# Streamed weights of a two-layer attention and mixer kernel: held output blocks, a shorter ring, and key and query loads in two transfers

## The chip, the cores and the metric

The kernel runs on one core of a Trainium2 chip. The metric is the device time of one execution in microseconds, the median of three runs. The profile is that of one execution, taken by the hardware profiler, and it is a little longer (3707.0 us) than the timed runs.

## The reference

A sequence of 2048 rows with 640 columns passes through attention, a mixer, and both a second time with the same weights. Each block adds its result to its input.

The attention block works on 64 segments of 32 rows, one after the other, with 8 memory rows ahead of each:

```
for s in range(n_seg):                     # 64 segments
    h = concat([mem, x[32 s : 32 s + 32]]) # 8 + 32 rows of 640
    q, k, v = h @ Wq, h @ Wk, h @ Wv       # 32 heads of 192 columns
    p = softmax(mask(q k^T * scale))
    o = (p v) @ Wo                         # 6144 -> 640
    mem = o[:8]                            # the next segment's memory
    outs.append(o[8:])
```

The memory rows of a segment are an output of the segment before, so the segments of one block can't be computed side by side. Wq, Wk, Wv and Wo have 640 x 6144 elements each, 7.9 MB in bfloat16, 31.5 MB together, and every segment needs all of them.

The mixer normalizes, multiplies by w1 (640 x 640), applies gelu, shifts four groups of columns by one or two rows up or down, multiplies by w2 (640 x 640), normalizes, multiplies by w3 (640 x 1536), applies gelu and multiplies by w4 (1536 x 640).

## The kernel before

**Steps and lanes.** The first attention (lane 0) and the second (lane 1) use the same weights, so the kernel runs them together: step t handles segment t of lane 0 and segment t - 5 of lane 1 (`LAG`). There are 69 steps. A step's activations hT are 2 x 40 = 80 columns wide. Each weight block is loaded into TensorE once per step and multiplied with these 80 columns. Every second step a chunk of the mixer (64 rows of both lanes) is worked off in between.

**Groups.** The 32 heads go in 8 groups of 4 (768 columns). For each group there is a projection of keys and of queries (`proj_kq`, 5 blocks of 128 rows each, 6 matmuls a block, line 526), one of values (`proj_v`, line 567, with a transposition at L579), then `attend`: scores (L598), softmax on VectorE and ScalarE, transposition (L631), product with the values (L646), copy to oT (L652), and the output projection (L663), 6 blocks of 5 matmuls, which adds into the tile psy. When all 8 groups have been added, L701 copies the memory rows out of psy into the next step's hT.

**Resident and streamed weights.** `CUT` says how many blocks of each group stay in SBUF for the whole run. Keys, queries and values keep 3 of 5 blocks in each group. The output weights keep 2, 4, 4, 4, 4, 4, 2, 2 of 6. The other blocks are streamed again in every step, two blocks to a load, into a ring of buffers of 128 x 1536 elements (`wst`). The ring has 10 buffers (`RING`). Attention may hold 9 (`RING_A`) and the mixer's weights, which are all streamed, 3 (`RING_B`). `block` (line 415) makes the attention loads: a resident one at L425, a streamed one at L435. `load_b` makes the mixer's at L459. All are issued by the SP queue, in order. SP waits before each load until TensorE has freed the buffer.

**The order of the work.** A planner in Python (`Plan.place`) orders everything by hand before the program is built. Each operation has an engine, a cost and a due time, and the planner puts at each point the operation that can start first and is due first. It also models the ring, with a rate, a latency and a skew of the loads (`DMA_RATE`, `DMA_LAT`, `DMA_SKEW`). A planned step is 48 us long (`STEP`). So a constant of the planner changes the order of instructions on every engine, and nothing else.

**Held output blocks.** The end of a step is a chain: the last groups' softmax, their output projection, the memory rows, and only then the next step's first keys. To give TensorE work in it, the output projections of groups 2 to 6 can be kept back: oT has 7 buffers (`OT_BUFS`), and the due time of these groups is the step's end (line 655). In the kernel before this holds for resident blocks alone. A streamed block is due two group lengths after its group began (line 671).

Of the kernel before, what the change touches and what calls it, by code (L numbers as in the profile page):

```python
# [19 lines left out]

LAG = 5
HG = 4
RING = 10
RING_A = 9
RING_B = 3
CUT = {"k": [3] * 8, "q": [3] * 8, "v": [3] * 8, "o": [2] + [4] * 5 + [2] * 2}
YA = 3
STEP = 48.0
PSUM_BANKS = {"y": 2, "x": 6}
PSUM_USES = {"y": ("y", 2), "P": ("x", 4), "S": ("x", 3), "B": ("x", 2)}  # L30
OT_BUFS = 7
# [4 lines left out]
LOOK = 0.03  # L36
DMA_RATE = 345.0e3
DMA_LAT = 2.2
DMA_SKEW = 2.8


class Buf:
# [194 lines left out]
def kernel(  # L237
# [16 lines left out]
    nc = tc.nc  # L254
    P = 128
# [6 lines left out]
    KC = Dm // P  # L262
    FC = F // P
    assert (Dm, F, Dh, H, SEG, M) == (640, 1536, 192, 32, 32, 8) and S % (2 * SEG) == 0 and NSEG > 8
    NG = H // HG
    GW = HG * Dh
    GC = GW // P
# [108 lines left out]
    add = plan.add  # L376
# [9 lines left out]
    def T(b):  # L386
        if b.obj is None:
            b.obj = b.make()
        return b.obj

    def mm_us(n, m=128, k=1):
        return k * (max(min(64, m), n) / 2400.0 + 0.0025)
# [9 lines left out]
    def w_src(kind, g, a, e):  # L402
        if kind == "o":
            return Wo_v[:, g, a:e, :]
        return W_v[kind][:, a:e, GW * g:GW * (g + 1)]
# [9 lines left out]
    def block(t, kind, g, c, due):  # L415

        n = Dm if kind == "o" else GW
        cut = CUT[kind][g]
        if c < cut:
            if (kind, g) not in resident:  # L420
                tl = wres.tile([P, cut, n], bf16, name=f"w{kind}{g}")
                b = Buf()

                def fn(op):
                    nc.sync.dma_start(out=tl[:], in_=w_src(kind, g, 0, cut))  # L425
                add("SP", 0.45, due, fn, w=(b,), dma=P * cut * n * 2, queue="wa")
                resident[kind, g] = b, tl
            b, tl = resident[kind, g]
            return b, lambda: tl[:, c, :]
        a = cut + (c - cut) // 2 * 2  # L430
        if (t, kind, g, a) not in streamed:
            b = ring("ra")

            def fn(op):
                nc.sync.dma_start(out=T(b)[:, 0:2 * n].rearrange("p (c n) -> p c n", c=2), in_=w_src(kind, g, a, a + 2))  # L435
            add("SP", 0.45, due, fn, w=(b,), dma=P * 2 * n * 2, queue="wa")
            streamed[t, kind, g, a] = b
        b = streamed[t, kind, g, a]
        return b, lambda: T(b)[:, (c - a) * n:(c - a + 1) * n]
# [62 lines left out]
    def attention_step(t):  # L502
# [3 lines left out]
        N = NS if both else L1  # L506
        maskt = mask2[:] if both else (mask_a if 0 in ln else mask_b[:])
        base = t * STEP
        sl = STEP / NG
# [77 lines left out]
        def attend(g):  # L587
            G = t * NG + g
            s0 = base + sl * g
            q, k_, V_ = qT[G % 2], kT[G % 2], Vt[G % V_BUFS]  # L590
# [60 lines left out]
            def f7(op):  # L651
                nc.vector.tensor_copy(out=o_[:, :, 0:N], in_=T(pso)[:, :, 0:N])  # L652
            add("DVE", dve_us(GC * N), hi - 4, f7, r=(pso,), w=(B("oT", G % OT_BUFS),))
            ws = [block(t, "o", g, c, s0 + (1.9 if g < NG - 1 else 1.2) * sl + 0.03 * c) for c in range(GC)]
            due = base + STEP - 1 + 0.02 * g if g >= NG - OT_BUFS + 1 else s0 + 2.0 * sl

            def out_rows(m0, m1, c0_, c1_, j):

# [7 lines left out]
            if g < NG - 1:  # L666
                for c in range(GC):
                    def f8(op, c=c):
                        out_rows(0, YA, c, c + 1, 0)()
                        out_rows(YA, KC, c, c + 1, 1)()  # L670
                    add("PE", mm_us(N, k=KC), due if c < CUT["o"][g] else s0 + 2.0 * sl, f8,
                        r=(ws[c][0], B("oT", G % OT_BUFS)), a=tuple(psy))
            else:
                for j, (m0, m1) in enumerate(((0, YA), (YA, KC))):
                    def f8(op, j=j, m0=m0, m1=m1):
                        out_rows(m0, m1, 0, GC, j)()
                    add("PE", mm_us(N, k=GC * (m1 - m0)), due + 0.5 * j, f8,
                        r=(*{id(b): b for b, _ in ws}.values(), B("oT", G % OT_BUFS)), a=(psy[j],))
# [5 lines left out]
        g = NG - 2  # L684
# [7 lines left out]
        due = base + STEP - 5  # L692
# [11 lines left out]
        for j, (k0, k1) in enumerate(((0, YA), (YA, KC))):  # L704
            def fy(op, j=j, k0=k0, k1=k1):
# [5 lines left out]
                a=() if j == 0 else (B("yTB", t % 2),))  # L711
# [123 lines left out]
    def chunk(c):  # L835
# [108 lines left out]
            gelu(pz, e - a, i, due, outs, (B("hTB", i),))  # L944
        hs = [ps("B", [XB, HC], f32, "hs") for _ in range(2)]
        for n in range(5):
            due = D(0.4 + 0.04 * n)
            wb, wv = load_b(c, "w2", n, due)

            def fw(op, n=n, wv=wv):  # L950
                w = wv()
                off = W2OFF[n] if n < 4 else 0
                lhsT = hTB[:, n, off:off + TOK, :].rearrange("p w l -> p (w l)")
                for k in range(2):
                    nc.tensor.matmul(out=T(hs[k])[:], lhsT=lhsT, rhs=w[:, HC * k:HC * (k + 1)],  # L955
                                     start=hs[k].begin(), stop=True, skip_group_check=True)
            add("PE", mm_us(HC, k=2), due, fw, r=(wb, B("hTB", 0), B("hTB", 1)), a=tuple(hs))
# [19 lines left out]
        for i in range(4):  # L977
            a, e = 3 * i, 3 * i + 3
            pz = ps("B", [P, 3, XB], f32, "psh2")
            for n in range(a, e):  # L980
                due = D(0.7 + 0.04 * n)
                wb, wv = load_b(c, "w3", n, due)

                def fw(op, n=n, a=a, wv=wv, pz=pz):
                    w, o = wv(), T(pz)
                    for kc in range(KC):
                        nc.tensor.matmul(out=o[:, n - a, :], lhsT=w[:, kc * P:(kc + 1) * P],  # L987
                                         rhs=vT[:, kc, 0:XB], start=(kc == 0), stop=(kc == KC - 1))
                add("PE", mm_us(128, k=KC), due, fw, r=(wb, vTk), a=(pz,))
            gelu(pz, 3, i % 2, due, [(0, P, 0, 3, h2T[:, a:e, :])], (B("h2T", i),))  # L990

    def chunk_end(c):
        base = (2 * c + 2) * STEP
        D = lambda x: base + x * STEP
        xk, vk = B("xw"), B("vb")
        s4k = B("st", 3)
        y2 = [ps("B", [XB, HC], f32, "y2") for _ in range(2)]
        for n in range(FC):
            due = D(1.2 + 0.03 * n)
            wb, wv = load_b(c, "w4", n, due)  # L1000

            def fw(op, n=n, wv=wv):
                w = wv()
                for k in range(2):
                    nc.tensor.matmul(out=T(y2[k])[:], lhsT=h2T[:, n, :], rhs=w[:, HC * k:HC * (k + 1)],  # L1005
                                     start=y2[k].begin(), stop=True, skip_group_check=True)
            add("PE", mm_us(HC, k=2), due, fw, r=(wb, *(B("h2T", k) for k in range(4))), a=tuple(y2))
        for k in range(2):
            def fs(op, k=k):
                cs = slice(HC * k, HC * (k + 1))  # L1010
                nc.vector.scalar_tensor_tensor(out=xo[:, cs], in0=T(y2[k])[:], scalar=0.5, in1=xw[:, cs],
                                               op0=ALU.mult, op1=ALU.add)
            add("DVE", dve_us(HC), D(1.5), fs, r=(y2[k], xk), w=(B("xo"), B("fin")) if k == 0 else (),
                a=() if k == 0 else (B("xo"), B("fin")))
        for lane in range(2):
            w0 = rows_of(c, lane)
            a, b = max(0, -w0), min(TOK, S - w0)
            if b <= a or a >= TOK:
                continue

            def fst(op, lane=lane, a=a, b=b, w0=w0):
                dst = x2d if lane == 0 else outd
                nc.gpsimd.dma_start(out=dst[w0 + a:w0 + b, :], in_=xo[2 * a + lane:2 * b:2, :])
            add("POOL", 0.9, D(1.55), fst, r=(B("xo"),), w=(B("x2d", c),) if lane == 0 else (), dma=(b - a) * Dm * 2)
        segs = [(2 * c - 1, 0, 2, 30, "xc"), (2 * c, 2, 2 + SEG, 0, "xa"), (2 * c + 1, 2 + SEG, TOK, 0, "xb")]
        segs = [x for x in segs if 0 <= x[0] < NSEG]
        if segs:
            st_ = st4[3]
            ln_ops(xo, XB, st_, s4k, B("xo"), D(1.5), False)
            apply_ln(vb, xo, XB, st_, 0, vk, B("xo"), s4k, D(1.5), 0.45)  # L1030
            ps4 = ps("B", [P, KC, XB], bf16, "psn")
            transposes(ps4, vb, XB, D(1.5), (vk,))
            for (sg, a, b, o0, key) in segs:
                tt = sg + LAG

                def fc(op, a=a, b=b, o0=o0, tt=tt):
                    pv = T(ps4)[:].rearrange("p k (w l) -> p k l w", l=2)
                    d0 = L1 + M + o0
                    nc.scalar.copy(out=hT[tt % 4][:, :, d0:d0 + b - a], in_=pv[:, :, 0, a:b])
                add("ACT", act_us(KC * (b - a)), D(1.55) + (0.0 if o0 else 1.0), fc, r=(ps4,), w=(B("hT", tt % 4, key),))  # L1040
        if c + 1 < NCH:
            chunk_loads(c + 1)
# [81 lines left out]
```

## Time and profile before

| | before |
|---|---|
| median of 3 runs | 3685.22 us (3682.99 to 3686.92) |
| span of the profiled run | 3707.0 us |
| TensorE matmul busy | 3410.3 us (92%), 84,703 matmuls |
| VectorE, ScalarE, GpSimd busy | 2362.8, 1710.7, 308.2 us |
| moved by DMA | 1141.77 MB, mean 308 GB/s |
| of it by the SP queue | 1113.63 MB |
| streamed attention loads | 759 output, 552 key, 552 query, 552 value |
| mixer loads | 630 |
| median time of a streamed load from issue to landing | 5.5 to 5.9 us |

Busy time of TensorE is a modelled figure, since matmuls overlap, so 92% doesn't say that it runs at its peak. A wait is listed as engine, line, what ended it, then the sum in us, the number of waits and the longest one. "Issue" is put where the engine stood still and the profile shows nothing that it waited for. A queue's share of 16 engines is the time of its packets divided by 16 times the span.

### The profile page before, as it was taken

The page shows a single profiled execution, that of the slowest core. Times are in us where ns is not written, and L with a number is a line of the kernel's source. Part 1 is how long each engine was busy: PE and PEld are TensorE (multiplying, and loading weights), DVE is VectorE, ACT ScalarE, POOL GpSimd, SP SyncE. Part 2 cuts the span into 40 slices and gives each one's busy share as a digit, 9 for nine tenths or more (in the row PEclk, how much of TensorE's full clock was granted, in tenths as well). Part 3 has the DMA queues.
Part 4 walks back from the last instruction along what each step waited for, and adds up shares of the span by engine and source line. Part 5 has one row for each costly group of instructions (what it writes and reads, how often), then busy time and mean ns, then how long its engine had stood idle before and what let it go on. Part 6 is the DMA issues. An engine that isn't in the chain of part 4 may idle for free.

```text
span 3707.0 us, 188581 instructions
## 1 busy us (share of the span) xinstructions
PE 3410.3 (92%) x84703; PEld 3273.5 (88%) x84703; DVE 2362.8 (64%) x7085; ACT 1710.7 (46%) x3584; POOL 308.2 (8%) x522
## 2 busy tenths in 40 slices
PE   5889999999999999999999999999999999999896
PEld 4778999999999999999998999988999999898785
DVE  2455666766666666666666666666666667666455
ACT  1344444444444544444444445444445445444333
POOL 2000000000000000000000000000000000000000
PEclk9999999999999999999999999999999999999898
DMA  9999999999999998999999999999899999999996
GB/s 343 320 305 303 311 313 308 307 307 305 316 307 322 321 313 296 304 311 317 305 308 304 318 310 307 313 307 309 291 314 318 311 306 309 298 315 313 298 322 217
DMA packets 841818, 1141.77 MB, mean 308 GB/s; under 512 B 54190, under 2 KB 837564, under 8 KB 841008
## 3 DMA queue, kind: packets, MB, share of 16 engines
q1 hardware_dynamic: 832496, 1113.63, 90.6%
q0 software_dynamic: 8512, 16.08, 1.2%
q8 instruction: 662, 10.85, 1.2%
q14 instruction: 148, 1.21, 0.1%
HBM read 1124.25 MB, written 8.19 MB: 305 GB/s over the span
## 4 chain that ended last, share of the span: by engine, by line
PE 88%; issue 7%; DMA 3%; ACT 1%; DVE 1%; SPq 0%; POOL 0%; POOLq 0%; DVEq 0%; ACTq 0%
PE psq L526 16%; PE psk L526 15%; PE psy L663 15%; PE psv L567 15%; PE psvt L579 5%; PE pss L598 4%; PE pso L646 4%; PE psh L987 3%; PE y L1005 3%; PE pst L631 2%; DMA wst<-in_A_Wq_dram 1%; PE psh L933 1%; PE hs L955 1%; DMA wst<-in_A_Wv_dram 1%; ACT V L583 1%
## 5 line engine op out<-in xcount | busy, mean ns | idle before, releaser
L652 DVE CAST oT<-pso 128x480 bf16<-128x480 f32 (+1 forms) x552 | 340.9, 618 | 396.6 <-PE pso L646 393.1
L526 PEld LDWEIGHTS <-wst 128*128 128x128 bf16 x13248 | 548.6, 100 | 47.4 <-issue 30.1
L583 ACT COPY V<-psvt 80x768 bf16<-80x768 bf16 (+1 forms) x552 | 438.5, 794 | 298.9 <-PE psvt L579 298.3
L526 PE MATMUL psq<-hT,wq 128*128 128x80 bf16 (+1 forms) x9936 | 475.9, 199 | 51.2 <-issue 21.2
L526 PE MATMUL psk<-hT,wk 128*128 128x80 bf16 (+1 forms) x9936 | 474.6, 199 | 38.8 <-issue 29.8
L573 ACT CAST vTs<-psv 128x480 bf16<-128x480 f32 (+1 forms) x552 | 292.0, 529 | 458.4 <-PE psv L567 458.0
L567 PE MATMUL psv<-hT,wv 128*128 128x80 bf16 (+1 forms) x9936 | 481.0, 199 | 18.7 <-issue 17.1
L609 DVE CUSTOM_DVE_ANT_1 pss<-pss,mask 80x320 f32<-80x320 f32 (+1 forms) x512 | 245.8, 480 | 380.2 <-PE pss L598 376.5
L534 ACT CAST qT<-psq 128x480 bf16<-128x480 f32 (+1 forms) x552 | 292.7, 530 | 405.4 <-PE psq L526 404.0
L526 PEld LDWEIGHTS <-wq 128*128 128x128 bf16 x9936 | 411.1, 100 | 69.3 <-issue 49.4
L526 PEld LDWEIGHTS <-wk 128*128 128x128 bf16 x9936 | 400.7, 100 | 45.8 <-issue 40.6
L663 PE MATMUL psy<-oT,wo 128*128 128x80 bf16 (+1 forms) x8970 | 414.6, 199 | 24.1 <-issue 17.5
L567 PEld LDWEIGHTS <-wv 128*128 128x128 bf16 x9936 | 402.9, 100 | 34.7 <-issue 21.9
L636 ACT COPY PT<-pst 80x320 bf16<-80x320 bf16 (+1 forms) x552 | 221.8, 402 | 385.3 <-PE pst L631 377.3
L663 PE MATMUL psy<-oT,wst 128*128 128x80 bf16 (+1 forms) x7590 | 379.1, 199 | 20.7 <-issue 16.0
L663 PEld LDWEIGHTS <-wo 128*128 128x128 bf16 x8970 | 358.4, 100 | 35.2 <-issue 26.0
L567 PE MATMUL psv<-hT,wst 128*128 128x80 bf16 (+1 forms) x6624 | 356.8, 199 | 21.5 <-issue 19.2
L526 PE MATMUL psk<-hT,wst 128*128 128x80 bf16 (+1 forms) x6624 | 346.7, 200 | 19.0 <-issue 13.9
L621 DVE TENSOR_REDUCE sm<-pss 80x4 f32<-80x320 f32 (+1 forms) x552 | 252.6, 458 | 172.4 <-ACT pss L616 171.7
L663 PEld LDWEIGHTS <-wst 128*128 128x128 bf16 x7590 | 317.9, 100 | 37.0 <-issue 24.9
L526 PE MATMUL psq<-hT,wst 128*128 128x80 bf16 (+1 forms) x6624 | 324.1, 199 | 16.0 <-issue 11.6
L542 DVE CAST kT<-psk 128x320 bf16<-128x320 f32 (+1 forms) x552 | 253.7, 460 | 122.1 <-PE psk L526 121.4
(117 smaller groups left out, 5285.2 us busy)
## 6 DMA issues: line engine op xcount, KB each, us to landing
wst<-in_A_Wo_dram SPq DMA_DIRECT2D x759, 320.0 KB, 5.5
wst<-in_A_Wk_dram SPq DMA_DIRECT2D x552, 384.0 KB, 5.9
wst<-in_A_Wq_dram SPq DMA_DIRECT2D x552, 384.0 KB, 5.7
wst<-in_A_Wv_dram SPq DMA_DIRECT2D x552, 384.0 KB, 5.7
wst<-wbd SPq DMA_DIRECT2D x280, 320.0 KB, 5.8
wst<-in_B_w_dram SPq DMA_DIRECT2D x280, 320.0 KB, 5.7
wst<-wbd SPq DMA_DIRECT2D x70, 160.0 KB, 5.7
wk<-in_A_Wk_dram SPq DMA_DIRECT2D x8, 576.0 KB, 10.3
```

What stands on the lines that cost most here:

```text
L526: nc.tensor.matmul(out=o[:, c, 0:N], lhsT=w[:, c * P:(c + 1) * P], rhs=h[:, kc, c0:c0 + N], start=pq.begin(), stop=True, skip_group_check= ...
L534: nc.scalar.copy(out=q[:, :, 0:N], in_=T(pq)[:, :, 0:N])
L542: nc.vector.tensor_copy(out=k4[:, :, 0::3, 0:N], in_=p4[:, :, 0::2, 0:N])
L567: nc.tensor.matmul(out=o[:, c, 0:N], lhsT=w[:, c * P:(c + 1) * P], rhs=h[:, kc, c0:c0 + N], start=pv.begin(), stop=True, skip_group_check= ...
L573: nc.scalar.copy(out=vs[:, :, 0:N], in_=T(pv)[:, :, 0:N])
L579: nc.tensor.transpose(out=T(pt)[0:N, c, :], in_=vs[:, c, 0:N], identity=ident[:, :])
L583: nc.scalar.copy(out=V_[0:N, :, 0:Dh], in_=T(pt)[0:N].rearrange("n c f -> n (c f)").rearrange("n (i e) -> n i e", i=HG))
L609: nc.vector.tensor_tensor_reduce(out=o, in0=o, in1=maskt.unsqueeze(1).to_broadcast([N, HG, N]), scale=-scale, scalar=3.0e38, op0=ALU.add, ...
L621: nc.vector.reduce_sum(out=sm_[0:N, 4:4 + HG], in_=o, axis=AX.X)
L636: nc.scalar.copy(out=Pt[0:N, :, 0:N], in_=T(pst)[0:N, :, 0:N])
L652: nc.vector.tensor_copy(out=o_[:, :, 0:N], in_=T(pso)[:, :, 0:N])
L663: nc.tensor.matmul(out=T(psy[j])[:, m - m0, c0:c0 + N], lhsT=w[:, m * P:(m + 1) * P], rhs=o_[:, c, 0:N], start=psy[j].begin(), stop=True, ...
```

## The change

It has four parts.

- **Ring and resident blocks.** The ring shrinks from 10 buffers to 8, and attention may hold 7. The space goes to output weights: groups 6 and 7 now keep 4 of 6 blocks.
- **Held groups.** For groups 2 to 6 the streamed output blocks are due at the step's end too, and their loads are due a little ahead of it (`HOLD`).
- **w4 late.** The mixer's last product is due 0.3 of a step later. The due times of w2 and w3 become named constants with the values that they had.
- **Key and query loads.** Each streamed load of these two is issued as two transfers, the first for partitions 0 to 119, the second for partitions 120 to 127. The planner's skew falls from 2.8 to 2.4 us.

What it is for: more of the weights stay in SBUF, work is shifted to places where TensorE might wait, and the bytes of a load are divided over the DMA engines in another way.

```diff
-RING = 10
-RING_A = 9
+RING = 8
+RING_A = 7
 RING_B = 3
-CUT = {"k": [3] * 8, "q": [3] * 8, "v": [3] * 8, "o": [2] + [4] * 5 + [2] * 2}
+CUT = {"k": [3] * 8, "q": [3] * 8, "v": [3] * 8, "o": [2] + [4] * 7}
...
+HOLD = 4.0
+W3 = (0.7, 0.04)
+W4 = (1.5, 0.025)
+W2 = (0.4, 0.04)
...
-DMA_SKEW = 2.8
+DMA_SKEW = 2.4
...
-                nc.sync.dma_start(out=T(b)[:, 0:2 * n].rearrange("p (c n) -> p c n", c=2), in_=w_src(kind, g, a, a + 2))
-            add("SP", 0.45, due, fn, w=(b,), dma=P * 2 * n * 2, queue="wa")
+                o, i = T(b)[:, 0:2 * n].rearrange("p (c n) -> p c n", c=2), w_src(kind, g, a, a + 2)
+                if kind in ("k", "q"):
+                    nc.sync.dma_start(out=o[0:120], in_=i[0:120])
+                    nc.sync.dma_start(out=o[120:P], in_=i[120:P])
+                    return
+                nc.sync.dma_start(out=o, in_=i)
+            add("SP", 0.9 if kind in ("k", "q") else 0.45, due, fn, w=(b,), dma=P * 2 * n * 2, queue="wa")
...
-            ws = [block(t, "o", g, c, s0 + (1.9 if g < NG - 1 else 1.2) * sl + 0.03 * c) for c in range(GC)]
-            due = base + STEP - 1 + 0.02 * g if g >= NG - OT_BUFS + 1 else s0 + 2.0 * sl
+            held = g >= NG - OT_BUFS + 1
+            at = base + STEP - HOLD + 0.5 * g if held else s0 + 1.9 * sl
+            ws = [block(t, "o", g, c, at + 0.03 * c) for c in range(GC)]
+            due = base + STEP - 1 + 0.02 * g if held else s0 + 2.0 * sl
...
-                    add("PE", mm_us(N, k=KC), due if c < CUT["o"][g] else s0 + 2.0 * sl, f8,
+                    add("PE", mm_us(N, k=KC), due, f8,
...
-            due = D(1.2 + 0.03 * n)
+            due = D(W4[0] + W4[1] * n)
             wb, wv = load_b(c, "w4", n, due)
```

More of the change, by code (lines that the diff above doesn't have):

```diff
@@ L946, in chunk @@
         for n in range(5):
-            due = D(0.4 + 0.04 * n)
+            due = D(W2[0] + W2[1] * n)
             wb, wv = load_b(c, "w2", n, due)
@@ L980, in chunk @@
             for n in range(a, e):
-                due = D(0.7 + 0.04 * n)
+                due = D(W3[0] + W3[1] * n)
                 wb, wv = load_b(c, "w3", n, due)
```

## The prediction

> **What bounds the kernel now.** I read the page's totals first, then the waits of TensorE, then the stretches of the span, then one stall in the timeline, and last the waits of the SP queue.
>
> ```profile
> PE 3410.3 (92%) x84703; PEld 3273.5 (88%) x84703; DVE 2362.8 (64%) x7085; ACT 1710.7 (46%) x3584; POOL 308.2 (8%) x522
> ...
> q1 hardware_dynamic: 832496, 1113.63, 90.6%
> ...
> q8 instruction: 662, 10.85, 1.2%
> ...
> PE 88%; issue 7%; DMA 3%; ACT 1%; DVE 1%; SPq 0%; POOL 0%; POOLq 0%; DVEq 0%; ACTq 0%
> ```
> TensorE is the path: 88% of the chain is its own work and 7% "issue", where it stood still though nothing in the program held it. Vector and Scalar work is far from full. The weight queue q1 fills 90.6% of the 16 DMA engines, and q8 is a small queue that carries instructions: 10.85 MB are 169,500 instructions of 64 bytes, and TensorE has 2 x 84,703 = 169,406. So q8 is TensorE's program.
>
> ```profile
> PEld L526 <- issue: 120.1, 142, 2.5
> PEld L663 <- issue: 50.9, 65, 2.1
> PEld L567 <- issue: 42.0, 50, 2.4
> PEld L598 <- issue: 13.2, 19, 1.5
> PEld L526 <- DMA wst<-in_A_Wk_dram: 6.0, 9, 2.7
> ```
> These are TensorE's longest waits: issue at every kind of matmul, some 250 us in all, and next to nothing for weights.
>
> ```profile
> 0.00:110.00 110.00, 62.90 (x1257) 51.09 (x1258) 22.46 (x95) 20.17 (x50) 26.18 (x49) 1.00 1.01 347
> 420.00:1900.00 1480.00, 1401.07 (x34758) 1364.75 (x34756) 998.23 (x2900) 720.45 (x1473) 117.71 (x198) 1.00 0.94 311
> ```
> Stretches of the span: the last three figures are clock, DMA share and GB/s. While the resident weights come in, the core moves 347 GB/s; in the steady part 311. So the sum of all engines' bandwidth does not bound the steady part, though the mean engine counts 94% busy.
>
> ```profile
> 2592.97 0.42 ACT L636 COPY PT<-pst 80x320 bf16<-80x320 bf16 x1
> 2595.52 0.15 PEld L526 LDWEIGHTS <-wk 128*128 128x128 bf16 x3 [2.54 <-issue]
> ```
> One stall: TensorE is inside a key projection with resident weights and stops for 2.54 us. By the packet records a q8 packet ran from 2593.02 to 2594.07 and the one before it had ended at 2586.60. I looked at all gaps over 0.3 us between starts of weight loads: 234 of them end 1.15 to 1.6 us after a q8 packet ended, and they sum to 224.7 us. TensorE waits for its own program.
>
> A q8 packet holds 256 instructions, 128 matmuls with their loads, which TensorE works off in 128 x 36 ns (the usual distance of two loads) = 4.6 us. A packet takes 1.05 us (median) and about 1.35 us more until TensorE goes on. After a stall ends, the next packet starts 1.14 us later at the 5th percentile and 2.58 us at the median. It stalls TensorE if it starts later than 4.6 - 2.4 = 2.2 us. The 1.1 us are its own latency, so the rest, 1.5 us at the median, is queueing behind weights.
>
> ```profile
> SPq L435 <- PE psq L526: 353.5, 294, 2.7
> SPq L435 <- DMA wst<-in_A_Wo_dram: 5.0, 11, 0.6
> ```
> SP, which issues the weights in order, waits for TensorE to free a buffer and hardly for landings.
>
> [...] The trace before shows only 16 landings for each 128-partition load. [...] The trace has no engine numbers.
>
> **Does one engine carry the fetches?** The q8 packets never overlap, and take 706 us together. For weight loads in whose flight a q8 packet falls, the last of 16 shares lands 0.49 us after the 15th (median); for others 0.20. So a fetch delays one share: one engine. At the median packet times (55 ns for each of 350,088 packets of 1280 B, 65 ns for each of 433,152 of 1536 B) the weights take 1203 + 1760 = 2963 us of each engine. With fetches the hot one has 2963 + 706 = 3669 us, about the whole span of 3685.
>
> **The change, part by part.**
> *The split.* 552 + 552 streamed key and query loads have 256 packets of 1536 B. An engine now takes 16 of each, 1104 x 16 x 0.065 = 1148 us in all. [...]
> *More resident.* Groups 6 and 7 keep four output blocks of six instead of two: 2 loads fewer in each of 69 steps, 138 x 16 packets x 55 ns = 121 us less on every engine, and 45 MB less in all.
> Sum at about 3540 us: engine 15 with the fetches 2963 - 1148 - 121 + 706 = 2400 us (68%), engines 0 to 7 2986 us (84%), the others 2842 us. Nothing is full.
> *What this is worth.* Weights then occupy (2400 - 706) / 3540 = 48% of engine 15 instead of 2963 / 3685 = 80%. If queueing shrinks in that ratio, 40% of each fetch's delay beyond 1.1 us goes. Taken off the 234 stalls one by one this leaves 38 us, a gain of 187; at 30% it leaves 71. The most is all 225. Some stalls hide other waits, so I take 80%: 150 us.
> *SP.* 1104 more issues less 138: an issue takes 368 ns and the next follows about 0.1 us later, so SP goes from 3079 x 0.46 = 1416 to 4045 x 0.46 = 1861 us, 53%. It stays on the side. The second issue of a pair delays what is queued behind it by 0.46 us, under the lead below.
> *New landing waits.* In the built program the loads share eight semaphores in turn, and an issue waits until the load eight before it landed. Eight are now 5.8 loads of data. At today's issue times with pairs 0.46 us apart, 14% of issues would come less than 5.2 us after the one eight before, against a median landing of 5.7. But then 5 or more loads, each over 1 us of every engine, are queued, so the engines do not run dry. Cost: none on the path.
> *Ring of 8.* Ten buffers for 3045 streamed loads give 10 x 3685 / 3045 = 12.1 us for a buffer's round; eight for 2907 give 8 x 3540 / 2907 = 9.7. Less 5.7 us of flight, lead plus use falls from 6.4 to 4.0 us. TensorE now waits some 30 us for streamed weights. At best no more is added; at worst the 5% of loads that take 7.7 us, 2 us over the median, stop it by about 1 us each, 145 us. I take 15, since 2 us late is less than 4.0.
> *Held groups.* The streamed output blocks of groups 2 to 6 move to the step's end with the resident ones, up to 10 matmuls each between the last softmax stages. The waits there are short (TensorE for the memory copy L701: 4.4 us, for oT: 4.3), so I take 10 us of gain, between 0 and 20. Their loads go in a row through SP, with the next step's key and query loads queued behind them; that is in the 15.
> *w4 late.* Its 24 matmuls a chunk end 0.25 step (some 13 us) later, 0.27 step before the next chunk needs their result. Attention matmuls fill the time: nothing.
> Sum: 3685 - 150 - 10 + 15 = 3540.
>
> **Rivals.**
> *Loads take the place of fetches* (20%). Fetches get through, but a faster TensorE with 2.4 us less lead waits for weights and takes 100 of the 150 back: 3640. For it: the engines' 94% and the runs of output loads. Against: 347 GB/s at the start, 4% fewer bytes.
> *The fetches are on one of engines 8 to 14* (8%). Then only 121 of its 3669 us go, about 4% of the delay: 22 us by the same list of stalls. 3685 - 22 - 10 + 15 = 3668. For it: the trace names no engine.
> *They are on one of 0 to 7, slower* (17%). That engine goes to 2986 + 706 = 3692 us, full: the stalls stay and grow, loads' last shares come later into a shorter ring. 3685 + 23 + 30 = 3738. [...] Ring waits of the worst size without relief belong here too.
>
> **How the numbers follow.** My forecast, fetches on 15 and relieved, has 55%[...], and gains are also had elsewhere. The time is 3540. Its low end is 3685 - 225 - 20 = 3440, of which I cut a little: 3450. The high end takes in the rivals at 3640 and 3668 and the mild half of the slow case: 3700. That leaves out about 2 in 10. Faster: 55 + 20 + 6 = 81%; same 3%; slower 16%.
>
> **What would show it.** Right: issue falls from 7% of the chain to 2 or 3%, the weight loads' waits for issue at L526 from 120 to under 40 us, q1 down to about 1068 MB at a similar GB/s. Waits for streamed weights below 60 us mean that the ring suffices; over 130 us, the first rival. Issue unchanged means the fetches are not on engine 15; issue grown, the slow case. The forecast is wrong if a 15-engine transfer itself is slower, which nothing here shows: then the key and query loads' time to landing would rise above 5.9 us.

## The result and the profile after

The changed kernel takes 4368.09 us (median of 4 runs, 4340.53 to 4394.1) against 3684.1 us (median of 4): a ratio of 1.1855, interval 1.1777 to 1.1932. It moves 45 MB less and takes 684 us more.

The page of the changed kernel: span, TensorE, the weight queue, the fetch queue, and the chain by engine.

```profile
span 4338.8 us, 190574 instructions
...
PE 3599.6 (83%) x84703; PEld 3404.8 (78%) x84703; DVE 2392.2 (55%) x7085; ACT 1708.1 (39%) x3584; POOL 305.1 (7%) x522
...
q1 hardware_dynamic: 803200, 1069.09, 97.0%
...
q8 instruction: 667, 10.93, 1.2%
...
PE 49%; DMA 41%; issue 9%; SPq 1%; ACT 0%; DVE 0%; POOL 0%; POOLq 0%; DVEq 0%; ACTq 0%
```

The limit lies elsewhere now. Before, DMA was 3% of the chain; now it is 41%. The weight queue takes 97.0% of the engines' time, where it took 90.6%, for fewer bytes in a longer span. The waits of TensorE's weight loads, longest first:

```profile
PEld L535 <- issue: 208.3, 172, 3.8
PEld L535 <- DMA wst<-in_A_Wk_dram: 91.3, 100, 2.9
PEld L576 <- issue: 87.5, 67, 3.7
PEld L1016 <- issue: 83.2, 79, 2.6
PEld L674 <- issue: 72.2, 73, 3.8
PEld L576 <- DMA wst<-in_A_Wv_dram: 55.2, 71, 2.0
```

The wait for streamed key weights went from 6.0 to 91.3 us. All waits for streamed weights, those of weight loads and of matmuls counted together though they overlap, went from some 31 to 432 us. Waits put down to "issue" grew too. Those at L1016 are not waits for instructions, though: its matmuls waited 74.0 us for streamed mixer weights, with the weight loads behind them. The same steady stretch as before, with clock, DMA share and GB/s last:

```profile
420.00:1900.00 1480.00, 1258.38 (x29652) 1207.78 (x29649) 862.99 (x2474) 610.88 (x1253) 100.39 (x169) 0.97 1.00 254
```

DMA share 1.00 at 254 GB/s, where it was 0.94 at 311: the engines are busy all the time and move less. So each packet must take longer. The packet records say so: a packet of 1536 bytes had a median of 65 ns and a mean of 73, and now has 100 and 102. Packets of 1280 bytes, whose loads weren't touched, went from a mean of 61 to 71 (62 in the run e1 below, which has the rest of the change without the split). The SP queue shows the same from its side, since it now waits for landings of earlier loads, where before it had only 5.0 us on its longest row of that kind:

```profile
SPq L442 <- DMA wst<-in_A_Wk_dram: 168.6, 163, 2.4
SPq L441 <- PE psy L674: 168.2, 179, 2.5
SPq L444 <- DMA wst<-in_A_Wq_dram: 166.4, 177, 2.5
```

Below, "fetch stalls" (TensorE waiting for its own program) is the sum of those gaps of TensorE that end 1.15 to 1.6 us after a packet of q8, counted as in the prediction. They went from 224.7 to 402.2 us.

### The profile page after: what moved, and what is told of

Its sections match the earlier page's. It is cut to its first block, busy times and chain, and to the rows that moved or that the text cites. A ratio compares the mean times of both kernels' runs of the same rounds, so it can differ in the third digit from the quotient of the medians.

```text
span 4338.8 us, 190574 instructions
## 1 busy us (share of the span) xinstructions
PE 3599.6 (83%) x84703; PEld 3404.8 (78%) x84703; DVE 2392.2 (55%) x7085; ACT 1708.1 (39%) x3584; POOL 305.1 (7%) x522
## 4 chain that ended last, share of the span: by engine, by line
PE 49%; DMA 41%; issue 9%; SPq 1%; ACT 0%; DVE 0%; POOL 0%; POOLq 0%; DVEq 0%; ACTq 0%
DMA wst<-in_A_Wk_dram 13%; PE psy L674 11%; DMA wst<-in_A_Wq_dram 11%; PE psv L576 8%; PE psq L535 8%; DMA wst<-in_B_w_dram 8%; PE psk L535 7%; DMA wst<-in_A_Wv_dram 5%; PE psvt L588 3%; PE pso L655 2%; PE pss L607 2%; PE psh L998 2%; DMA wst<-wbd 1%; PE pst L640 1%; PE y L1016 1%
## 5 line engine op out<-in xcount | busy, mean ns | idle before, releaser
L674 PE MATMUL psy<-oT,wo 128*128 128x80 bf16 (+1 forms) x10350 | 513.9, 201 | 45.6 <-issue 39.1
L535 PEld LDWEIGHTS <-wk 128*128 128x128 bf16 x9936 | 412.0, 101 | 78.5 <-issue 60.9
L674 PEld LDWEIGHTS <-wo 128*128 128x128 bf16 x10350 | 429.9, 101 | 53.0 <-issue 43.7
L535 PE MATMUL psk<-hT,wst 128*128 128x80 bf16 (+1 forms) x6624 | 363.2, 203 | 122.4 <-DMA wst<-in_A_Wk_dram 77.6
L576 PEld LDWEIGHTS <-wv 128*128 128x128 bf16 x9936 | 412.2, 101 | 64.8 <-issue 52.6
L535 PE MATMUL psq<-hT,wst 128*128 128x80 bf16 (+1 forms) x6624 | 341.8, 202 | 70.1 <-issue 40.9
L674 PE MATMUL psy<-oT,wst 128*128 128x80 bf16 (+1 forms) x6210 | 354.3, 202 | 28.1 <-issue 25.5
```

Source lines behind the costliest of these rows:

```text
L535: nc.tensor.matmul(out=o[:, c, 0:N], lhsT=w[:, c * P:(c + 1) * P], rhs=h[:, kc, c0:c0 + N], start=pq.begin(), stop=True, skip_group_check= ...
L576: nc.tensor.matmul(out=o[:, c, 0:N], lhsT=w[:, c * P:(c + 1) * P], rhs=h[:, kc, c0:c0 + N], start=pv.begin(), stop=True, skip_group_check= ...
L674: nc.tensor.matmul(out=T(psy[j])[:, m - m0, c0:c0 + N], lhsT=w[:, m * P:(m + 1) * P], rhs=o_[:, c, 0:N], start=psy[j].begin(), stop=True, ...
```

## Experiments

### The split taken out, put in alone, and made in another way

**e1**: the changed kernel, each key and query load one transfer again. The planner's cost for such a load goes back from 0.9 to 0.45 us with it.

```diff
-                o, i = T(b)[:, 0:2 * n].rearrange("p (c n) -> p c n", c=2), w_src(kind, g, a, a + 2)
-                if kind in ("k", "q"):
-                    nc.sync.dma_start(out=o[0:120], in_=i[0:120])
-                    nc.sync.dma_start(out=o[120:P], in_=i[120:P])
-                    return
-                nc.sync.dma_start(out=o, in_=i)
-            add("SP", 0.9 if kind in ("k", "q") else 0.45, due, fn, w=(b,), dma=P * 2 * n * 2, queue="wa")
+                nc.sync.dma_start(out=T(b)[:, 0:2 * n].rearrange("p (c n) -> p c n", c=2), in_=w_src(kind, g, a, a + 2))
+            add("SP", 0.45, due, fn, w=(b,), dma=P * 2 * n * 2, queue="wa")
```

> The changed kernel with each key and query load as one transfer of 128 partitions again; ring, resident blocks, held groups, w4 and the planner's constants as changed. Shape theory (the 120-partition transfer is slow in itself): 1536-byte packets return to a 65 ns median, time at or below before, 3560 to 3680 us. Count theory (two transfers for a load eat SP time and the eight semaphores): also 3560 to 3680. Ring theory (eight buffers are too few, loads come late): stays above 4000 us with over 200 us of waits for streamed weights.

Measured: 3601.02 us, ratio 0.9768 (0.974 to 0.9796). Packets of 1536 bytes are back at a median of 65 ns, and waits for streamed weights add up to some 28 us, in the same count as the 432. The ring theory falls.

**e2**: the kernel before with the two transfers of 120 and 8 partitions alone.

> The kernel before with the two transfers of 120 and 8 partitions alone. Shape theory: about as slow as the changed kernel or slower, since there are 4 percent more bytes, 4350 to 4550 us, packets at a 100 ns median. Count theory: slower too, 4000 to 4400, but packets at 65 ns and SP waits for landings. Ring theory: 3500 to 3750 us.

Measured: 4630.43 us, ratio 1.2565 (1.2517 to 1.2613), the worst of all, and above the 4350 to 4550 that the shape theory gave. Packets of 1536 bytes took 98 ns (median). The split alone carries the loss, and the rest of the change softens it.

**e3**: two transfers for a load still, but one for each block, both of 128 partitions.

```diff
-                    nc.sync.dma_start(out=o[0:120], in_=i[0:120])
-                    nc.sync.dma_start(out=o[120:P], in_=i[120:P])
+                    nc.sync.dma_start(out=o[:, 0:1], in_=i[:, 0:1])
+                    nc.sync.dma_start(out=o[:, 1:2], in_=i[:, 1:2])
```

> The changed kernel with each key and query load in two transfers still, but one for each of its two blocks, both of 128 partitions: the same number of issues and semaphores, another shape. Shape theory: close to the unsplit one, 3580 to 3720 us, packets at 65 ns. Count theory: as slow as the changed kernel, above 4200 us. Ring theory: above 4000.

Measured: 3549.03 us, ratio 0.9624 (0.9601 to 0.9647). As many issues and as many turns of the eight semaphores as in the changed kernel, and 819 us less. The count theory falls. Not foreseen: it is also faster than one transfer (3601). The planner's cost differs between these two (0.9 against 0.45 us) and can change the order of the work, so the 52 us need not all come from the transfers. The changed kernel, e3, e11, e13 and e14 have the same planned order and differ in the two transfers alone.

### Shapes by themselves

**e4** leaves out all of the reference's computation and loads one shape again and again, with eight buffers (one execution). Its loop, shortened; the special shapes and the wait at the end of each stretch are left out:

```python
for name, count, pairs in PHASES:          # e.g. name = ((0, 120), (120, 128))
    for i in range(count):
        for p0, p1 in name:
            nc.sync.dma_start(out=buf[i % 8][p0:p1, 0:2, 0:768], in_=W[p0:p1, 3:5, ...])
    pe(pairs)                              # free matmuls: load weights, multiply
```

> No attention and no mixer, an output of zeros: ten stretches of 40 loads (60 in the third), all of 1536-byte rows (3072 in the third) into eight buffers, one shape to a stretch: 128 partitions; 120; 8; 112; 96; 64; 60; 120 and 8; 112 and 16; two transfers of one block and 128 partitions each; beside them TensorE runs matmuls without a data dependence all the time, and at the end without loads. Shape theory[...]: 128 near 345 GB/s, 120 near 220 to 260, 64 and 60 at 217 or below, 112 and 96 between. [...] Count theory: the two-transfer stretches all fall, the single 120 does not. [...]

Stretches of e4, last figure GB/s: 128 partitions, then 120, 112, 96, 64, then 120 and 8, 112 and 16, and block by block.

```profile
41.00:70.00 29.00, 21.23 (x575) 20.72 (x572) 0.00 (x0) 0.00 (x0) 1.00 1.04 369
80.00:134.00 54.00, 36.09 (x893) 35.38 (x890) 0.00 (x0) 0.00 (x0) 0.94 1.02 249
280.00:329.00 49.00, 35.61 (x833) 35.00 (x830) 0.00 (x0) 0.00 (x0) 0.88 1.08 266
336.00:381.00 45.00, 33.37 (x823) 32.76 (x820) 0.00 (x0) 0.00 (x0) 0.92 1.08 249
388.00:425.00 37.00, 29.74 (x764) 29.13 (x761) 0.00 (x0) 0.00 (x0) 0.95 1.10 200
475.00:542.00 67.00, 56.24 (x1490) 55.33 (x1487) 0.00 (x0) 0.00 (x0) 0.97 0.97 229
549.00:606.00 57.00, 50.43 (x1373) 49.51 (x1370) 0.00 (x0) 0.00 (x0) 1.00 1.05 267
612.00:660.00 48.00, 45.87 (x1258) 45.25 (x1255) 0.00 (x0) 0.00 (x0) 1.00 0.93 297
```

128 partitions move 369 GB/s, 120 only 249. It isn't a matter of 15 landing records in place of 16, as a load of 120 leaves them: 15/16 of 369 would be 346 GB/s, and 112, which keep 16 (counted in e11), come to 266. The DMA share is about 1 in all of them, so each packet got slower (in these stretches a median of 66 ns for 128, 99 for 120 and 112, 105 for 96, 133 for 64).

The stream of matmuls shows the fetches alone: under 128-partition loads four of five pages of 128 matmuls end in a gap of 1.93 us (the first in 1.13), block by block in gaps of 0.3 to 1.1 us or in none, and without loads in none. The stretch of 8 partitions had gaps of 8 to 10 us, but only at 4 of its 20 fetches, so loads of 8 partitions hold up some fetches and not others. In the stretch of 120 the gaps were mostly 2.0 to 3.3 us: loads with 15 landing records in place of 16 relieve nothing.

**e5** puts the same number of partitions in different places. It too computes nothing of the reference (one execution).

> No attention and no mixer, an output of zeros: stretches of loads of one shape, beside them TensorE runs matmuls without a data dependence. First seven stretches of 40: 128 partitions; 64 neighbours; 64, every second; 16 neighbours; 16, every eighth; 32 neighbours; 32, every fourth (the last four with ten times 1536 bytes a partition). [...] 64 neighbours 190 GB/s, every second one about 250; 16 neighbours [...] 95 to 110, [...] about 190; [...] about 190, every fourth [...] over 300. If the number of partitions decides and not their place: each pair alike. Then four stretches of 80 loads on 1, 2, 4 and 8 partitions[...]: the first of them in which TensorE's issue stalls come back, of 5 us and more, names the smallest set that holds the engine of the fetches; in the stretches before it TensorE should run free.

Stretches of e5: 64 neighbours, 64 every second; 16 neighbours, 16 every eighth; 32 neighbours, 32 every fourth.

```profile
77.00:113.00 36.00, 29.31 (x753) 28.80 (x750) 0.00 (x0) 0.00 (x0) 0.95 1.10 201
121.00:148.00 27.00, 27.00 (x760) 27.00 (x757) 0.00 (x0) 0.00 (x0) 1.00 0.85 262
156.00:242.00 86.00, 38.98 (x792) 38.37 (x789) 0.00 (x0) 0.00 (x0) 0.72 1.05 110
251.00:297.00 46.00, 30.85 (x709) 30.34 (x705) 0.00 (x0) 0.00 (x0) 0.85 1.04 200
305.00:399.00 94.00, 58.37 (x1293) 57.35 (x1291) 0.00 (x0) 0.00 (x0) 0.85 1.03 204
407.00:454.00 47.00, 36.51 (x989) 35.70 (x986) 0.00 (x0) 0.00 (x0) 1.00 1.03 398
```

With the number of partitions the same, their place decides: 32 neighbours 204 GB/s, 32 spread out 398; 16 neighbours 110, 16 spread out 200. 64 neighbours come to 201, about as much as 32 neighbours and 16 spread out. The second stretch (64 spread out, 262) was not full (share 0.85), with packets at 65 ns; SP issued its loads one after another, some 0.65 us apart. Each load of all six left 16 landing records, so the number of shares is the same. Packets of 3072 bytes took 124 ns (median) on 32 partitions spread out, 246 on 32 neighbours, 252 on 16 spread out and 456 on 16 neighbours: each step about doubles the time. Why the place has this effect was not shown.

The last stretches of e5 don't name the engine of the fetches: beside 1, 2 and 4 partitions TensorE ran without a stop, and in the one with 8 the matmuls had run out.

### The place of the partitions in the kernel itself

**e11** cuts at 112 instead of 120. Both transfers then leave 16 landing records (64,712 in all: 16 for every transfer, and 8 for the load of 8 memory rows).

> The changed kernel with key and query loads cut at 112 instead of 120 partitions, so that both transfers use all 16 engines [...]. [...] still far slower than before, packets at a 90 to 100 ns median; from the 258 against 221 GB/s of the shape stretches 3800 to 4100 us. If the added load on the fetches' engine is the main cause: 3550 to 3700.

Measured: 4193.83 us, ratio 1.1401 (1.1382 to 1.142). That is above the expected 3800 to 4100. Cutting at 112 took back 174 us of the 819 between the changed kernel and e3; 645 us remain, though every transfer of weights has 16 shares again.

**e13 and e14** cut into 64 and 64.

```diff
-                    nc.sync.dma_start(out=o[0:120], in_=i[0:120])
-                    nc.sync.dma_start(out=o[120:P], in_=i[120:P])
+                    nc.sync.dma_start(out=o[0:P:2], in_=i[0:P:2])     # e13; e14: 0:64
+                    nc.sync.dma_start(out=o[1:P:2], in_=i[1:P:2])     # e13; e14: 64:P
```

> The changed kernel with each key and query load as two transfers of 64 partitions, the even ones and the odd ones. Both transfers run on all 16 engines [...]. [...] packets at 65 ns, and about the time of the kernel with two one-block transfers, 3530 to 3590 us. If any transfer of fewer than 128 partitions is slow: above 4000 us.

> The same with the lower and the upper 64 partitions: the same number of transfers, sizes and engines[...]. [...] packets of 1536 bytes well above 65 ns and over 3900 us; from 195 GB/s for 64 neighbours, if the pair runs one half after the other for two fifths of the bytes, 4200 to 4700. If the place of the partitions doesn't matter: as the even and odd ones.

Measured: e13 3614.12 us, ratio 0.9827 (0.9796 to 0.9858); e14 4368.76 us, ratio 1.1879 (1.1839 to 1.192). The steady stretch, e13 and then e14:

```profile
420.00:1900.00 1480.00, 1434.26 (x35600) 1397.26 (x35596) 1032.27 (x2977) 735.00 (x1511) 122.37 (x204) 1.00 0.93 305
```

```profile
420.00:1900.00 1480.00, 1261.22 (x29606) 1209.10 (x29604) 860.70 (x2469) 612.92 (x1258) 101.31 (x170) 0.97 1.01 253
```

Number and size of the transfers are the same, both have 16 landing records for each, and SP takes 0.60 us for an issue in both; 755 us lie between them. e14 shows the picture of the changed kernel, engines full at 253 GB/s. So the place of the partitions decides, and neither the number of transfers nor their size. e13 came out slower than the expected 3530 to 3590.

Two things stay open. e4 has 120, 112 and 96 neighbours at 249 to 266 GB/s; that such a range is slow is shown, why it is slow is not. And each of these cuts picks other rows of the weights in DRAM along with other partitions of SBUF. No run moves one without the other.

### Where the fetches run

**e10** loads ever more partitions beside a stream of matmuls, and computes nothing of the reference (one execution).

> No attention and no mixer, an output of zeros: stretches of 40 loads on 4, 5, 6, 7, 8 and 16 partitions[...], beside a stream of free matmuls. The stalls for fetches begin with the first set that holds the fetches' engine. They were absent with 4 and up to 9.8 us long with 8, so they begin at 5, 6, 7 or 8. [...]

Stretches of e10: 5 partitions, 7, 8, 16. The second column of figures, matmul busy time, falls short of the stretch by the gaps.

```profile
115.00:200.00 85.00, 85.00 (x2377) 85.00 (x2375) 0.00 (x0) 0.00 (x0) 1.00 0.30 37
300.00:389.00 89.00, 76.22 (x1993) 76.02 (x1990) 0.00 (x0) 0.00 (x0) 0.92 0.45 51
394.00:483.00 89.00, 69.77 (x1852) 69.57 (x1849) 0.00 (x0) 0.00 (x0) 0.88 0.53 57
488.00:564.00 76.00, 34.21 (x727) 33.70 (x724) 0.00 (x0) 0.00 (x0) 0.76 1.05 111
```

No gap with 4 and 5 partitions, one with 6, two each with 7 and 8, and with 16 six. With 16 the six are in a row (number 88 to 93 of the run), with 7 and with 8 it is two neighbours (62 and 63, then 78 and 79). In the stretch of 8 partitions of e4 they were 20 and 21, then 28 and 29. If all fetches were served by one engine, and the loads of a stretch all ran on the same ones, either all fetches of a stretch or none should have been held up. So I read this as fetches on more than one engine; it was not shown directly. In the kernel before, the stalls, sorted by the number of the fetch modulo 16, fall into all 16 classes (9 to 22 in each). Which engine serves which fetch stays open.

### Smaller shares, and the other parts of the change

> The changed kernel, but key, query and value loads each as two transfers of one block and 128 partitions. Fetch theory (a fetch waits for the share of each queued load on its engine, 16 packets, and for 8 when loads are halved): stalls on fetches fall from 104 us to 60 to 90, time 3505 to 3545 us. If something else made the two-block-wise kernel faster (first block usable earlier): about 3549 or slower, since SP gets 552 issues more and fewer bytes are in flight.

> The same with the streamed output loads in two transfers too, so all attention loads. Fetch theory: fetch stalls 40 to 80 us, 3480 to 3540 us unless SP becomes the limit. SP theory: with some 5200 issues of 0.46 us and eight semaphores for half loads, loads come late, and the time rises above 3560.

> The kernel before with key and query loads as two transfers of one block and 128 partitions, nothing else. Fetch theory: the fetch stalls of 225 us fall by a quarter to a half, and the time by about as much: 3590 to 3640 us. If halved loads gain only with the other parts: 3670 to 3690.

> The kernel before with the ring of 8 and groups 6 and 7 resident to four blocks alone; no held streamed blocks, w4 and the planner's skew as before, loads unsplit. If the fewer loads alone gave the gain of the unsplit kernel: 3590 to 3620 us. If the held groups and w4 gave it: 3660 to 3690. If the shorter ring costs by itself and the held groups repay it: above 3690.

> Held groups, w4 late and the skew of 2.4 as in the changed kernel, with the ring of 10 and the resident blocks of before, loads unsplit. With the kernel before, the unsplit one (3601) and the one with the ring alone (3669) it makes a table of two by two. If the two parts add up, it lies at 3685 - 68 = about 3617 us. If the held groups only repay what the resident blocks of groups 6 and 7 take from the step's end, it lies at 3670 to 3690.

e6 and e7 are e3 with the condition on "k" and "q" widened to "v" (e6) and to all streamed attention loads (e7). e12 is the kernel before with e3's two lines. In these three, as in e3, the planner's cost of a load cut in two is 0.9 us. e8 is the kernel before with `RING`, `RING_A` and `CUT` of the change. e9 has everything but these and the split, so the planner's skew of 2.4 us too. Each ratio is to the kernel before as it ran beside that run, at 3682 to 3689 us.

| kernel | median us | ratio to before (interval) | fetch stalls us |
|---|---|---|---|
| before | 3684.1 | | 225 |
| e12: before, key and query by block | 3617.23 | 0.982 (0.9794 to 0.9847) | 162 |
| e8: ring and resident blocks alone | 3669.11 | 0.9947 (0.9924 to 0.9969) | 154 |
| e9: held groups, w4 and skew alone | 3675.63 | 0.9981 (0.9967 to 0.9995) | 200 |
| e1: both | 3601.02 | 0.9768 (0.974 to 0.9796) | 140 |
| e13: both, even and odd halves | 3614.12 | 0.9827 (0.9796 to 0.9858) | 130 |
| e3: both, key and query by block | 3549.03 | 0.9624 (0.9601 to 0.9647) | 104 |
| e6: both, value too | 3521.32 | 0.9543 (0.9513 to 0.9573) | 65 |
| e7: both, all attention loads | 3544.79 | 0.9606 (0.9582 to 0.963) | 45 |

*By block.* Each further kind of load that is cut by block takes fetch stalls away, and the time follows, until the loads themselves come late. e7 lies just above the range of its fetch theory and below that of its SP theory. In it the waits for streamed weights are back. What the instructions on `wst` waited for, first in e6, then in e7 (us, times):

```profile
  issue: 30.8, 49
  DMA wst<-in_A_Wk_dram: 8.4, 19
```

```profile
  DMA wst<-in_A_Wk_dram: 35.9, 77
...
  issue: 19.1, 27
```

e6 beats both kernels. Why it does is only partly shown. A block-wise transfer has 128 packets for 16 landing records, 8 for each instead of 16, so a fetch should wait for less, and e4 shows that (gaps of at most 1.1 us, mostly 1.93 with whole loads). But e13's transfers also have 8 packets, and it gained only 10 us of stalls over e1 and no time. Its waits for streamed weights rose from 28 to 52 us, and an issue took 0.60 us of SP where e3's took 0.34 to 0.42. The first block's earlier landing may count as well, and so may the planner's cost; no run separates them.

*Two by two.* Ring and resident blocks alone give 0.5%, held groups, w4 and skew alone 0.2%, both 2.3%. What the output projection waited for goes far to explain the difference, in e8 and then in e1:

```profile
  issue: 111.1, 178
  DVE oT L652: 40.7, 65
```

```profile
  issue: 37.2, 69
  DMA wo<-in_A_Wo_dram: 9.4, 10
```

With more resident blocks alone, fetch stalls fall by 71 us, but the output projection now stands waiting for oT for 40.7 us (before: 4.3). Holding the streamed blocks back removes that wait (0.5 us in e1). e8's time lies where the held groups would have given the gain, but e9 shows that they alone are worth 7 us. The second reading of e9, that they repay what the resident blocks take from the step's end, fits its time and these waits. The two parts don't add up; they gain together.

## Why the prediction was wrong

**The failed step is the sum of engine time under "the split".** It put 1104 x 16 packets at 65 ns, today's median, for transfers that the trace before didn't show. Its engine numbers were my assumption: no trace numbers the engines. The packets came out at 100 ns, and the account at 16 engines x 97% of the span: "nothing is full" was false, everything was. At the means of the packets after (101.7 ns for 433,152, 71.4 ns for 315,272) the weights take 2753 + 1407 = 4160 us of each engine, where the sum had at most 2986. A part of the gap was there before: the sum took medians, 2963 us, but 90.6% of 3707.0 us, on the same page, are 3359.

The last paragraph of the prediction named a slower 15-engine transfer as the one thing that would make the forecast wrong, "which nothing here shows", and gave it no bound, no rival and no chance of its own. It should have had one: the streamed loads of the trace before all have 128 partitions, so their packet times say nothing about 120. Nor does any run here show which partitions an engine took.

Why the 120 are slow stays open. That a neighbouring range short of 128 is slow is what e4 and e11 show (99 ns a packet for 120 and 112 in e4, 66 for 128). The sign that the prediction named did come where it can be read: in e11 the median streamed transfer took 7.0 us to land, against 5.7 before.

**One engine for the fetches** was wrong as well. "A fetch delays one share" is true of one fetch, but I took it for the same engine each time. The 3669 us of a hot engine, the relief by 40% and both rivals on the engine's number rested on that. e10 has some fetches held up and others not, which one engine for all doesn't explain. The page spoke against it already: 3359 us of weights and 706 us of fetches on one engine are 4065 us, more than the span of 3707 (an estimate, since shares of up to 1.10 in e4 show that packet records can overlap a little). And the 55% for engine 15 rested on nothing that was shown: no run here names an engine or shows a slow one.

**What held.** TensorE waits for its own program. In e12 63 us of stalls and 67 us of time went, in e1 85 and 83. Stalls don't turn into time by themselves: in e8 71 us of them went and only 15 of time, while 40.7 us of waits for oT came up. The counts behind the sum were right too: the landing records of 4 bytes number 54,776, which is 1836 x 16 + 1104 x 15 + 1104 x 8 + 8, the last for the load of 8 memory rows. So a transfer of 120 partitions has 15 shares, and one of 8 has 8, with two packets in each: from there come the 144 us by which 2986 us exceed 2842 in the sum. Two transfers in place of one cost nothing on the path (e3), as the steps on SP and the semaphores said. So did the ring of 8: some 28 us of weight waits in e1 against some 30.

**Sizes.** Held groups were put at 10 us and measured 7 alone (0.19%, with w4 and the skew), but some 68 beside the resident blocks (3669 - 3601). Adding parts up hid that. The rivals all lay within 1.5% of before. Signs that were to tell them came, 432 us of weight waits for one and issue at 9% of the chain for another, but from a cause that neither had. The slower one's 3738 was right in sign and 630 us short, and right by luck: it had one engine full with fetches, where all 16 were full with slow packets (DMA share 1.00).

## What to carry to other kernels

Before cutting a load by partitions, run the pieces alone and read the time of one packet. Try it with other partitions of the same number too, since their place can decide: the same transfers over 64 neighbours instead of every second partition cost this kernel 755 us on 3614. Where a load has to be cut, try the free dimension, which keeps 128 partitions. For key and query loads that gained 1.4% beside the other parts of the change and 1.8% alone, the planner's new cost included. And when DMA engines look full, ask for the time of one packet before counting bytes.

## What the runs showed of the hardware

- With 16 landing records for each load, packets of 3072 bytes took 124 ns on 32 partitions, every fourth one; 246 on 32 neighbours; 252 on 16, every eighth; 456 on 16 neighbours (e5).
- Ranges of 120, 112 and 96 neighbouring partitions ran at 249 to 266 GB/s, 128 at 369 (e4).
- Beside slow transfers the others slowed too: packets of untouched 1280-byte loads went from 61 to 71 ns on average, and to 62 without the split (e1).
- Under full 128-partition loads instruction fetches stopped TensorE at each page, in most of them for 1.9 us after some 4.6 us of work (e4). Under loads on 16 neighbouring partitions, with packets of 3072 bytes, it was 8.4 to 9.4 us (e10).
- Loads of 8 partitions held up 4 of 20 fetches (e4) and two (e10), loads of 16 six in a row (e10). No trace shows which engine serves a fetch.
